# A mixture-of-experts kernel: its table of tokens by slot made by matmuls of zeros and ones in place of scatters, with attention and routing pieces reordered

## The chip, the cores and the metric

The kernel runs on one core of a Trainium2 chip. The metric is the device time of one execution in microseconds (us); the time of a version is the median over its runs. A core has five engines that run their own instruction streams and meet at semaphores: TensorE (PE, matmuls; PEld its weight loads), VectorE (DVE), ScalarE (ACT), GpSimd (POOL) and SyncE (SP, which mostly issues DMAs). An engine takes its instructions strictly in its own order.

## The reference

Three layers follow each other on B = 2 sequences of S = 768 tokens with 8 heads of 40. The first is a gated recurrent attention, computed here in chunks of 128 tokens. The second sends each token to 2 of 8 experts, the third adds four experts over all tokens:

```python
logits = x @ w_gate
noisy_logits = logits + np.log1p(np.exp(x @ w_noise)) * noise
top2 = np.argpartition(-noisy_logits, 2, axis=1)[:, :2]
...
for e in range(E):                       # 8 experts, F = 1024
    for k in range(2):
        mask = top2[:, k] == e
        h = np.maximum(x[mask] @ w1[e], 0.0)
        out[mask] += top2_w[mask, k, None] * (h @ w2[e])
...
for e in range(E):                       # 4 experts over all 1536 tokens
    h = np.maximum(x @ w1[e], 0.0)
    out += p[:, e:e + 1] * (h @ w2[e])
```

## The kernel before

**Stages.** Attention runs in 12 chunks, six of each batch. A chunk's row `x` goes to the table `Xall` in DRAM. Its scores `sp`, decays `A`, state update `up` and state `C`, output `hp`, `tp`, `x`, transposes `xp` and routing logits `lp`, `lt` are computed by all the engines in turn: PE makes the products, DVE multiplies scores into A, adds `up` to C and normalises `x`; ACT takes exponentials and copies; POOL masks A (`affine_select`, L335), scales queries (`qg`, L353) and decays C (L368). Routing of a batch (`route`) is done in two halves, h = 0 for its first four chunks and h = 1 for the last two. The first expert layer then runs in units: units 0 to 3 are experts 0 to 3 for the tokens of batch 0 alone (two tiles of 128), unit 4 and those behind it need tokens of batch 1. A unit gathers its tokens from `Xall` (`xload`, POOL indirect DMAs `xe`), transposes them (`prep`, into `pa`, `pb`), splits them into a high and a low part (`xh` on ACT, `xl` on DVE), multiplies by the first weights (L194, result `s`), takes the positive part and splits it (`hh`), and multiplies by the second weights (L208). Weights come as `raw` by SP's DMAs and are split as `w1hi`, `w2hi` on ACT and `w1lo`, `w2lo` on DVE (L174, L175).

**Order.** It is written out by hand in two strings. `PLAN1` mixes, up to unit 0, attention pieces (A, four to a chunk), routing pieces of batch 0 (r), weight splits (w) and single steps (z, o). What is left of routing and splits is then drained, the gathers of units 0 and 1 are issued, and `LEAD` further attention pieces are drained before unit 0 is prepared. `PLAN2` is woven with the matmuls of units 0 to 3, one letter or blank after each group of matmuls: A is the rest of attention, r the routing of batch 1. A scheduler then sets the order of instructions of one piece on the engines.

**The table.** Which token stands in which slot of which expert is known, for each token, as a slot number. `route` writes the number of each token to the DRAM table `Td` at its slot: 8 indirect DMAs by POOL for h = 0 and 4 for h = 1, a yield after each, so that each is an r of its own. After h = 1 SP reads the table back into `tok`, 32 columns of 128, and the gathers take their row numbers from `tok`.

Of the kernel before, what the change touches and what calls it, by code (L numbers as in the profile page):

```python
# [65 lines left out]
def body(ctx: ExitStack, tc: tile.TileContext, d, o, dbg=None):  # L66
    nc = tc.nc
    const = ctx.enter_context(tc.tile_pool(name="const", bufs=1))
# [28 lines left out]
    slot = [const.tile([P, 2, NC], I32, name=f"slot_{b}") for b in range(B)]  # L97
# [6 lines left out]
    Td = dram.tile([NROW, 1], I32, name="Td")  # L104
# [28 lines left out]
    toki = const.tile([P, NT], I32, name="toki")  # L133
    nc.gpsimd.iota(toki, pattern=[[P, NT]], base=0, channel_multiplier=1)
    zidx = const.tile([P, E1 * NCOL], I32, name="zidx")
    nc.gpsimd.memset(zidx, 0)
    dumpi = pro.tile([P, NC, E1], I32, name="dumpi")
    nc.gpsimd.iota(dumpi, pattern=[[P * E1, NC], [P, E1]], base=SPARE, channel_multiplier=1)
    dump = const.tile([P, NC, E1], F32, name="dump")
    nc.gpsimd.tensor_copy(dump, dumpi)  # L140
# [337 lines left out]
    def route(b, h):  # L478
        t = rt[b]
        if h == 0:  # L480
            nl = at.tile([P, NC, E1], F32, name="nl")
            selb = at.tile([P, NC, E1], BF16, name="selb")
            sel = at.tile([P, 2, NC, E1], F32, name="sel")
            t.update(nl=nl, selb=selb, sel=sel, prev=[])
        nl, selb, sel, prev = t["nl"], t["selb"], t["sel"], t["prev"]
# [29 lines left out]
        sl = at.tile([P, 2, HC, E1], F32, name=f"sl{h}")  # L515
# [534 lines left out]
```

## Time and profile before

| | us |
|---|---|
| runs | 710.33, 710.69, 712.83 |
| median | 710.69 |
| the profiled execution | 708.15 |
| its span, first to last instruction | 706.1 |
| PE busy in the span | 680.1 |
| DVE busy | 369.3 |
| ACT busy | 262.1 |
| POOL busy | 126.1 |

The profiled execution is 2.54 us below the median and has 2.05 us outside its span. The clock of PE granted over the span was 0.976 of full speed. Times in the rows below are us from the span's start; the idle time of an engine before an instruction stands in brackets with what ended it.

### The profile page before, as it was taken

To read this page: it belongs to the slowest core of one execution; us is meant where nothing else is said; L and a number is where in the kernel's file an instruction comes from. 1 tells how busy PE (TensorE), PEld (TensorE's weight loads), DVE (VectorE), ACT (ScalarE), POOL (GpSimd) and SP (SyncE) were. 2 spreads that over 40 slices of the span, in tenths; PEclk is the share of its full clock that TensorE was granted. 3 is DMA by queue.
4 is the path that set the end of the run, shared out by engine and by line. 5 is a ranking of instruction groups with operands and counts; after the bars stand their busy time and mean duration, and the time that the engine had idled before them with its cause. 6 is when DMAs were issued, how large, how long until landed. Compare 5 with 4: busy or idle time off the path is not lost.

```text
span 706.1 us, 11386 instructions
## 1 busy us (share of the span) xinstructions
PE 680.1 (96%) x4427; PEld 622.7 (88%) x4427; DVE 369.3 (52%) x787; ACT 262.1 (37%) x501; POOL 126.1 (18%) x183
## 2 busy tenths in 40 slices
PE   9898688999999999999999999999999999999997
PEld 6776577999899999999889899898898998989987
DVE  7868587877565664658756334412444224332141
ACT  5558446763453543545541223302233113121120
POOL 5544572142612101124023000000000000000000
PEclk9998779999999999999999999999999999999999
DMA  6889647665665444567662003100130001001011
GB/s 195 220 246 302 196 115 234 194 202 168 172 195 163 136 135 148 135 189 244 187 189 75 1 19 109 38 1 1 31 103 31 1 1 37 1 1 39 1 37 41
DMA packets 39946, 80.03 MB, mean 113 GB/s; under 512 B 9377, under 2 KB 16465, under 8 KB 39889
## 3 DMA queue, kind: packets, MB, share of 16 engines
q1 hardware_dynamic: 36496, 70.39, 33.2%
q0 software_dynamic: 3392, 8.86, 4.5%
q8 instruction: 37, 0.61, 0.4%
q14 instruction: 21, 0.16, 0.1%
HBM read 70.20 MB, written 9.04 MB: 112 GB/s over the span
## 4 chain that ended last, share of the span: by engine, by line
PE 79%; DMA 10%; DVE 5%; issue 2%; ACT 1%; POOL 1%; SPq 0%; ACTq 0%; DVEq 0%; POOLq 0%
PE z L194 25%; PE z L208 24%; PE s L194 12%; PE s L208 10%; DMA raw<-w 4%; DMA A<-LFd 2%; PE sp L342 1%; PE s L204 1%; DMA raw<-v 1%; DMA Td<-toki,slot 1%; DMA kp<-kT 1%; DVE w2lo L175 1%; PE lp L449 1%; PE hp L407 1%; POOL Td L540 1%
## 5 line engine op out<-in xcount | busy, mean ns | idle before, releaser
L211 ACT ACTIVATE hh<-z 128x512 fp32r<-128x512 f32 x96 | 57.1, 600 | 192.4 <-PE z L194 192.3
L208 PE MATMUL z<-w2hi,hh 128*128 128x320 f32 x384 | 118.6, 309 | 0.0
L208 PE MATMUL z<-w2hi,hl 128*128 128x320 f32 x384 | 118.3, 308 | 0.0
L208 PE MATMUL z<-w2lo,hh 128*128 128x320 f32 x384 | 118.3, 308 | 0.0
L194 PE MATMUL z<-x2h,w1hi 128*128 128x512 f32 x288 | 112.4, 390 | 0.0
L208 PE MATMUL s<-w2hi,hh 128*128 128x320 f32 x448 | 107.6, 312 | 1.7 <-ACT hh L211 0.9
L212 DVE SCALAR_TENSOR_TENSOR hl<-z,hh 128x512 fp32r<-128x512 f32 x96 | 65.8, 690 | 82.5 <-ACT hh L211 82.5
L194 PE MATMUL z<-x2h,w1lo 128*128 128x512 f32 x288 | 96.6, 389 | 0.0
L194 PE MATMUL s<-xh,w1hi 128*128 128x256 f32 (+1 forms) x288 | 84.5, 312 | 3.3 <-ACT xh L186 3.3
L175 DVE TENSOR_TENSOR w2lo<-raw,w2hi 128x640 fp32r<-128x640 f32 x60 | 49.6, 828 | 65.6 <-ACT w2hi L174 65.5
L208 PEld LDWEIGHTS s<-w2hi,hh 128*128 128x128 f32 x448 | 76.7, 188 | 2.8 <-ACT hh L211 1.2
L174 ACT CAST w2hi<-raw 128x640 fp32r<-128x640 f32 x60 | 43.5, 728 | 87.2 <-PE s L204 25.3
L194 PE MATMUL z<-x2l,w1hi 128*128 128x512 f32 x192 | 74.8, 390 | 0.0
L175 DVE TENSOR_TENSOR w1lo<-raw,w1hi 128x768 fp32r<-128x768 f32 x60 | 57.2, 957 | 29.8 <-ACT w1hi L174 29.2
L208 PEld LDWEIGHTS z<-w2lo,hh 128*128 128x128 f32 x384 | 72.1, 188 | 0.6
L208 PEld LDWEIGHTS z<-w2hi,hh 128*128 128x128 f32 x384 | 72.1, 188 | 0.5
L208 PEld LDWEIGHTS z<-w2hi,hl 128*128 128x128 f32 x384 | 72.1, 188 | 0.0
L194 PE MATMUL s<-xh,w1lo 128*128 128x256 f32 (+1 forms) x288 | 70.5, 309 | 0.0
L208 PE MATMUL s<-w2lo,hh 128*128 128x320 f32 x224 | 69.2, 309 | 0.0
L194 PEld LDWEIGHTS z<-x2h,w1lo 128*128 128x128 f32 x288 | 54.1, 188 | 11.3
L174 ACT CAST w1hi<-raw 128x768 fp32r<-128x768 f32 x60 | 49.9, 836 | 36.7 <-PE s L194 15.3
L194 PEld LDWEIGHTS z<-x2h,w1hi 128*128 128x128 f32 x288 | 54.0, 188 | 10.8
(188 smaller groups left out, 1025.0 us busy)
## 6 DMA issues: line engine op xcount, KB each, us to landing
raw<-w SPq DMA_DIRECT2D x44, 384.0 KB
raw<-w SPq DMA_DIRECT2D x44, 320.0 KB
raw<-v SPq DMA_DIRECT2D x16, 384.0 KB
A<-LFd SPq DMA_DIRECT2D x10, 512.0 KB
raw<-v SPq DMA_DIRECT2D x16, 320.0 KB
kv<-kv SPq DMA_DIRECT2D x12, 324.0 KB
Yd<-ys SPq DMA_DIRECT2D x8, 320.0 KB
qt<-qT SPq DMA_DIRECT2D x12, 208.0 KB
```

What stands on the lines that cost most here:

```text
L174: nc.scalar.copy(hi, raw)
L175: nc.vector.tensor_sub(lo, raw, hi.bitcast(F32))
L194: nc.tensor.matmul(out_ps, l, r, start=(i == 0), stop=(i == len(seq) - 1))
L204: nc.tensor.matmul(yp, both[f], r[:, k], start=(f == 0 and i == 0), stop=(f == NF - 1 and i == 1))
L208: nc.tensor.matmul(yp, l, r, start=(f == 0 and i == 0), stop=(f == NF - 1 and i == 2))
L211: nc.scalar.activation(hh, src, AF.Relu)
L212: nc.vector.scalar_tensor_tensor(hl, src, 0.0, hh.bitcast(F32), ALU.max, ALU.subtract)
L342: nc.tensor.matmul(sp[:, j, :], t["kp"][:, 4 * g + j, :], t["qt"][:, j, :], start=True, stop=True)
L407: nc.tensor.matmul(hp[64 * j : 64 * j + 41, p, :], t["kv"][:, 4 * j + p, D:], t["A"][:, 4 * j + p, :], start=False, stop=(p == 3))
L449: nc.tensor.matmul(lp[32 * k : 32 * k + 32], wgn[r, k, :], st[i]["xt"][r, k, :], start=True, stop=True)
L540: s = nc.gpsimd.indirect_dma_start(out=Td, out_offset=bass.IndirectOffsetOnAxis(ap=slot[b][:, k, c : c + 1], axis=0), in_=toki[:, b * NC + ...
```

## The change

The table is made on chip. For each half of a batch, DVE builds a one-hot row over the 128 places of a column (`oh`) for each of the K = 8 or 4 token choices, and a one-hot row over the 32 columns (`in_col`), which it multiplies by the token's partition number and by the token's base (`rh`). K matmuls add the products up in PSUM (`pt`), and two additions put them into `table`; after h = 1 a cast makes `tok`. `Td`, its clearing, the slot cast, the 12 scatters of a batch and the read-back are gone. `sl` and `sf` have a third plane, for the place in the column. `LEAD` is 2 in place of 6, and both plans are rewritten: PLAN1 has 32 A and 21 r in place of 35 and 32, and a letter X at which the gathers of units 0 and 1 are issued; PLAN2 has 23 A and 25 r in place of 20 and 40.

```diff
-LEAD = 6
+LEAD = 2
-PLAN1 = "AAAAAAAAAAAzAAoAAAArrwArAwArrrrrArArrrrwrAAArrrArrArAwrrArArAArrrrArrrArA"
-PLAN2 = "A AA  AA r A AAA r rr rr A  A AA Ar ArrrrrrrrrA Arr r  A rrrr   rr rrrrr rr  r Arr rArr r  r "
+PLAN1 = "AAAAAAAAAAAAAAoAAArArArwArArArwArArrArArwrArrArwrXArArrAr"
+PLAN2 = "AA AA AA AA A    AAr AAr AAr AAr r r r r Ar Ar Ar Ar r r r r Ar Ar rr r r r r r "
...
-        nc.vector.scalar_tensor_tensor(spare, g, 0.0, dump[:, n], ALU.is_ge, ALU.mult)
+        nc.vector.tensor_scalar(spare, g, 0.0, 1000.0, ALU.is_ge, ALU.mult)
...
-        nc.vector.tensor_mul(tmp, sel[:, :, n], sl[:, 0].unsqueeze(1).to_broadcast([P, 2, HC, E1]))
-        nc.vector.tensor_reduce(sf, tmp, AX.X, ALU.add)
-        nc.vector.tensor_copy(slot[b][:, :, n], sf)
-        yield
-        for c in range(c0, c0 + HC):
-            for k in range(2):
-                s = nc.gpsimd.indirect_dma_start(out=Td, out_offset=bass.IndirectOffsetOnAxis(ap=slot[b][:, k, c : c + 1], axis=0), in_=toki[:, b * NC + c : b * NC + c + 1], in_offset=None)
...
-                yield
+        for w in (0, 2):
+            nc.vector.tensor_mul(tmp, sel[:, :, n], sl[:, w].unsqueeze(1).to_broadcast([P, 2, HC, E1]))
+            nc.vector.tensor_reduce(sf[:, w], tmp, AX.X, ALU.add)
+        K = 2 * HC
+        oh = at.tile([P, K, P], BF16, name=f"oh{h}")
+        rh = at.tile([P, 2, K, E1 * NCOL], BF16, name=f"rh{h}")
+        in_col = at.tile([P, K, E1 * NCOL], BF16, name=f"in_col{h}")
+        nc.vector.tensor_tensor(oh, count.unsqueeze(1).to_broadcast([P, K, P]), sf[:, 2].rearrange("p k c -> p (k c)").unsqueeze(2).to_broadcast([P, K, P]), ALU.is_equal)
+        yield
+        nc.vector.tensor_tensor(in_col, count[:, : E1 * NCOL].unsqueeze(1).to_broadcast([P, K, E1 * NCOL]), sf[:, 0].rearrange("p k c -> p (k c)").unsqueeze(2).to_broadcast([P, K, E1 * NCOL]), ALU.is_equal)
+        nc.vector.tensor_scalar(rh[:, 0], in_col, place[:, 0:1], None, ALU.mult)
+        for k in range(2):
+            c = slice(k * HC, (k + 1) * HC)
+            nc.vector.tensor_mul(rh[:, 1, c], in_col[:, c], place[:, 1 + b * NC + c0 : 1 + b * NC + c0 + HC].unsqueeze(2).to_broadcast([P, HC, E1 * NCOL]))
+        yield
+        pt = psum([P, 2, E1 * NCOL], "pt")
+        for i in range(K):
+            nc.tensor.matmul(pt, oh[:, i], rh[:, :, i], start=(i == 0), stop=(i == K - 1))
+        nc.vector.tensor_add(table, table, pt[:, 0])
+        nc.vector.tensor_add(table, table, pt[:, 1])
+        if h == 1:
+            nc.vector.tensor_copy(tok[b].rearrange("p e j -> p (e j)"), table)
+            routed.add(b)
+        yield
...
-        nc.sync.dma_start(tok[b].rearrange("p e j -> p (e j)"), Td[: P * E1 * NCOL].rearrange("(p j) o -> p (j o)", p=P))
```

The places where the order of instructions moves follow, each before and then with the change. The first is POOL's row beside the attention of chunks 8 to 10, where C is the attention state (L368), A the masked decay, qg the scaled queries; in brackets are the semaphores that a row waits for, DMASW those of POOL's own transfers. Before:

```order
L353 TENSOR_TENSOR qg<-qt,gb 104x512 [waits DMAHW5_49,DMAHW6_49,DMAHW3_49,PE_49]
L335 AFFINE_SELECT A<-A 128x512 [waits Activation_49]
L540 DMA Td<-toki,slot_89 10240x1 [waits DVE_49]
L540 DMA Td<-toki,slot_89 10240x1 x7
L335 AFFINE_SELECT A<-A 128x512 [waits DMAHW5_49,PE_49,Activation_49]
L368 TENSOR_TENSOR C_190<-C_188,gb 40x4x41 [waits PE_49]
L368 TENSOR_TENSOR C_190<-C_188,gb 40x4x41 [waits DMASW3_49,DMASW4_49,DMASW2_49,DMASW5_49,DMASW1_49,DMASW6_49,DMASW0_49,DMASW7_49,DVE_49,Pool_49]
```

With the change:

```order
L353 TENSOR_TENSOR qg<-qt,gb 104x512 [waits DMAHW4_49,DMAHW5_49,DMAHW2_49,PE_49]
L335 AFFINE_SELECT A<-A 128x512 [waits Activation_49]
L335 AFFINE_SELECT A<-A 128x512 [waits DMAHW3_49,PE_49,Activation_49]
L368 TENSOR_TENSOR C_190<-C_188,gb 40x4x41 [waits DVE_49,PE_49]
L368 TENSOR_TENSOR C_190<-C_188,gb 40x4x41 [waits DVE_49,Pool_49]
```

The eight scatters are gone from between qg and C, and the second C row no longer waits for transfers of POOL.

The second place is PE's row at chunk 7, from its scores to its output; pt is the new table product. Before:

```order
L342 MATMUL sp_1041<-qt,kp_162 128x128 x4
L449 MATMUL lp_1046<-xt,wgn 32x128 x3
L415 MATMUL tp_1055<-ident,hs 128x105 x4
L400 MATMUL hp_1081<-qg,C_190 105x128 x4
L460 MATMUL lt_1092<-ident,ls 128x96
```

With the change:

```order
L449 MATMUL lp_1040<-xt,wgn 32x128 x3
L553 LDWEIGHTS oh_980
L553 MATMUL pt_1047<-rh_981,oh_980 128x64
...
L415 MATMUL tp_1060<-ident,hs 128x105
L553 LDWEIGHTS oh_980
L553 MATMUL pt_1047<-rh_981,oh_980 128x64
...
L415 MATMUL tp_1060<-ident,hs 128x105 x3
L400 MATMUL hp_1086<-qg,C_190 105x128 x4
```

Eight table matmuls now stand between lp and the last of tp.

The third place is PE's row where the first expert matmul (L194, to `s`) stands. Before, where sp_1429 are scores and hp_1474 the output of chunk 11:

```order
L342 MATMUL sp_1429<-qt,kp_164 128x128 x4
L407 MATMUL hp_1420<-A,kv 41x128 x8
L449 MATMUL lp_1452<-xt,wgn 32x128 x3
L415 MATMUL tp_1459<-ident,hs 128x105 x4
L400 MATMUL hp_1474<-qg,C_190 105x128 x4
L612 MATMUL pa_1483<-ident,xe 128x128 x2
L407 MATMUL hp_1474<-A,kv 41x128 x5
L194 MATMUL s_102_1501<-xh,w1hi 128x256
```

With the change, where sp_1423 are scores of chunk 10 and hp_1371 is the output of chunk 9:

```order
L407 MATMUL hp_1371<-A,kv 41x128 x8
L626 MATMUL pa_1380<-ident,xe 128x128 x2
L627 MATMUL pb_1381<-ident,xe 64x128
L626 MATMUL pa_1380<-ident,xe 128x128 x2
L627 MATMUL pb_1381<-ident,xe 64x128
L194 MATMUL s_90_1398<-xh,w1hi 128x256
L342 MATMUL sp_1423<-qt,kp_162 128x128 x3
L194 MATMUL s_90_1398<-xl,w1hi 128x256
```

The scores of chunk 10 and all of chunk 11 stand behind the first expert matmul here; before, chunks 10 and 11 stood ahead of it but for the last products and transposes of chunk 11.

## Rows read from the trace of the kernel before

**Rows 1.** The page: busy time of each engine, share, instructions.

```profile
PE 680.1 (96%) x4427; PEld 622.7 (88%) x4427; DVE 369.3 (52%) x787; ACT 262.1 (37%) x501; POOL 126.1 (18%) x183
```

**Rows 2.** Windows, 60.4 to 114 us: length, busy time by engine, clock, DMA share, GB/s.

```profile
60.40:71.40 11.00, 10.51 (x93) 8.28 (x91) 10.10 (x35) 8.17 (x20) 5.53 (x6) 0.78 1.00 292
71.40:77.40 6.00, 2.44 (x40) 1.81 (x40) 5.29 (x24) 4.77 (x12) 4.71 (x5) 0.85 0.92 246
77.40:86.00 8.60, 8.60 (x55) 7.28 (x52) 1.75 (x8) 1.54 (x2) 2.66 (x5) 0.51 0.65 208
86.00:100.00 14.00, 9.93 (x67) 8.10 (x63) 12.00 (x47) 6.74 (x21) 10.15 (x14) 0.63 0.28 65
100.00:114.00 14.00, 11.38 (x125) 9.07 (x124) 8.73 (x24) 4.94 (x12) 9.33 (x9) 1.00 0.78 242
sum 53.60, PE 42.86 PEld 34.54 DVE 37.87 ACT 26.17 POOL 32.38; mean PE 8.57 PEld 6.91 DVE 7.57 ACT 5.23 POOL 6.48
```

**Rows 3.** Timeline of POOL: start, length, instruction; in brackets the idle time before it.

```profile
...
68.00 1.22 POOL L540 DMA_INDIRECT Td<-toki,slot  x1 [0.83 <-DVE xt L442]
...
77.63 0.96 POOL L540 DMA_INDIRECT Td<-toki,slot  x1 [0.30 <-issue]
...
85.31 0.47 POOL L368 TENSOR_TENSOR C<-C,gb 40x164 f32<-40x164 f32 x1 [5.63 <-DMA Td<-toki,slot]
...
86.45 1.26 POOL L353 TENSOR_TENSOR qg<-qt,gb 104x512 f32<-104x512 f32 x1
...
```

**Rows 4.** Timeline of VectorE (DVE), 79 to 115 us.

```profile
...
79.71 0.32 DVE L389 TENSOR_TENSOR C<-up,C 40x164 f32<-40x164 f32 x1 [2.18 <-POOL C L368]
...
85.81 0.33 DVE L389 TENSOR_TENSOR C<-up,C 40x164 f32<-40x164 f32 x1 [4.67 <-POOL C L368]
...
86.70 1.04 DVE L526 SCALAR_TENSOR_TENSOR sl<-g,sl 128x16 f32<-128x16 f32 x1
...
114.11 0.69 DVE L187 TENSOR_TENSOR xl<-pa,xh 128x512 fp32r<-128x512 f32 x1 [2.72 <-ACT xh L186]
...
```

**Rows 5.** Timeline of TensorE (PE), 37 to 116 us.

```profile
...
37.69 1.13 PE L342 MATMUL sp<-qt,kp 104*128 104x128 f32 x8 [0.51 <-PE up L376]
...
38.75 0.74 PE L449 MATMUL lp<-xt,wgn 128*32 128x128 f32 x6
...
50.73 0.74 PE L449 MATMUL lp<-xt,wgn 128*32 128x128 f32 x6
...
68.55 0.74 PE L449 MATMUL lp<-xt,wgn 128*32 128x128 f32 x6
...
73.64 0.41 PE L438 MATMUL xp<-ident,x 128*128 128x128 f32 x2 [1.96 <-DVE x L428]
...
77.72 2.08 PE L342 MATMUL sp<-qt,kp 104*128 104x128 f32 x8
...
115.24 0.39 PE L194 MATMUL s<-xl,w1hi 128*128 128x256 f32 x1
...
```

**Rows 6.** Groups of VectorE by line and shape, 0 to 200 us: busy, mean ns.

```profile
...
L175 DVE TENSOR_TENSOR w1lo<-raw,w1hi 128x768 fp32r<-128x768 f32 x21 | 19.9, 957 | 4.9 <-ACT w1hi L174 4.6
...
L500 DVE TENSOR_TENSOR df<-nl 128x256 f32<-128x256 f32 x2 | 0.9, 426 | 0.0
...
L500 DVE TENSOR_TENSOR df<-nl 128x128 f32<-128x128 f32 x2 | 0.6, 292 | 0.1
...
L545 DVE TENSOR_TENSOR tmp<-sel,sl 128x64 f32<-128x64 f32 x2 | 0.4, 212 | 0.0
...
```

**Rows 7.** Groups of TensorE by line and shape, 0 to 180 us.

```profile
...
L514 PE MATMUL pp<-selb,ones 128*128 128x24 bf16 x2 | 0.4, 178 | 0.0
...
```

**Rows 8.** Window of the dense units 0 to 3, columns as in rows 2.

```profile
115.20:181.40 66.20, 65.34 (x508) 63.31 (x505) 50.95 (x140) 37.16 (x62) 18.91 (x19) 1.00 0.63 181
```

**Rows 9.** Timeline of TensorE at the start of unit 4.

```profile
...
180.21 0.44 PE L612 MATMUL pa<-ident,xe 128*128 128x128 f32 x2 [0.25 <-DMA xe<-Xall,tok]
...
181.36 0.73 PE L194 MATMUL s<-xh,w1hi 128*128 128x256 f32 x4 [0.61 <-ACT xh L186]
...
```

More of the change, by code (lines that the diff above doesn't have):

```diff
@@ L27 @@
 NCOL = 4
-SPARE = P * E1 * NCOL
-NROW = SPARE + S * E1
 TINY = 1.1754944e-38
@@ L32 @@
 NQ = 4
-LEAD = 6
+LEAD = 2
 PARTS = [slice(0, 1), slice(1, 2), slice(2, 4), slice(4, NC)]
 WARM = 11
-PLAN1 = "AAAAAAAAAAAzAAoAAAArrwArAwArrrrrArArrrrwrAAArrrArArrAwrrArArAArrrrArrrArA"
-PLAN2 = "A AA  AA r A AAA r rr rr A  A AA Ar ArrrrrrrrrA Arr r  A rrrr   rr rrrrr rr  r Arr rArr r  r "
+PLAN1 = "AAAAAAAAAAAAAAoAAArArArwArArArwArArArrArArwrArrArwrXArArrAr"
+PLAN2 = "AA AA AA AA A    AAr AAr AAr AAr r r r r Ar Ar Ar Ar r r r r Ar Ar rr r r r r r "
 RAW = 3 * F // NQ
@@ L96, in body @@
     wsel = [const.tile([P, 2, NC], F32, name=f"wsel_{b}") for b in range(B)]
-    slot = [const.tile([P, 2, NC], I32, name=f"slot_{b}") for b in range(B)]
     back = [const.tile([P, 2, NC], I32, name=f"back_{b}") for b in range(B)]
@@ L103, in body @@
     psm = const.tile([P, NT], F32, name="psm")
-    Td = dram.tile([NROW, 1], I32, name="Td")
     tok = [const.tile([P, E1, NCOL], I32, name=f"tok_{b}") for b in range(B)]
@@ L132, in body @@
         nc.gpsimd.memset(off[b][:, ALONE:], -float(JCAP))
[L133 to L140, printed above, removed]
+    counti = pro.tile([P, P], I32, name="counti")
+    nc.gpsimd.iota(counti, pattern=[[1, P]], base=0, channel_multiplier=0)
+    count = at.tile([P, P], F32, name="count")
+    nc.gpsimd.tensor_copy(count, counti)
+    placei = pro.tile([P, 1 + NT], I32, name="placei")
+    nc.gpsimd.iota(placei[:, 0:1], pattern=[[0, 1]], base=0, channel_multiplier=1)
+    nc.gpsimd.iota(placei[:, 1:], pattern=[[P, NT]], base=0, channel_multiplier=0)
+    place = at.tile([P, 1 + NT], F32, name="place")
+    nc.gpsimd.tensor_copy(place, placei)
+    table = at.tile([P, E1 * NCOL], F32, name="table")
+    nc.gpsimd.memset(table, 0.0)
     STREAM = []
@@ L483, in route @@
             sel = at.tile([P, 2, NC, E1], F32, name="sel")
-            t.update(nl=nl, selb=selb, sel=sel, prev=[])
-        nl, selb, sel, prev = t["nl"], t["selb"], t["sel"], t["prev"]
+            t.update(nl=nl, selb=selb, sel=sel)
+        nl, selb, sel = t["nl"], t["selb"], t["sel"]
         n = HALVES[h]
@@ L514, in route @@
             nc.tensor.matmul(pp[:, j - c0 :, :], ones, selb[:, j - i : last + 1 - i, :], start=False, stop=(i == last))
-        sl = at.tile([P, 2, HC, E1], F32, name=f"sl{h}")
+        sl = at.tile([P, 3, HC, E1], F32, name=f"sl{h}")
         yield
@@ L526, in route @@
             nc.vector.scalar_tensor_tensor(sl[:, 0], g, float(i * P), sl[:, 0], ALU.is_ge, ALU.add)
-        nc.vector.scalar_tensor_tensor(sl[:, 0], sl[:, 0], float(1 - P * E1 * NCOL), wide(ebase[:, 0]), ALU.mult, ALU.add)
-        nc.vector.scalar_tensor_tensor(sl[:, 0], g, float(E1 * NCOL), sl[:, 0], ALU.mult, ALU.add)
-        nc.vector.tensor_max(sl[:, 0], sl[:, 0], spare)
+        nc.vector.scalar_tensor_tensor(spare, sl[:, 0], -float(P), spare, ALU.mult, ALU.add)
+        nc.vector.tensor_add(sl[:, 2], g, spare)
+        nc.vector.tensor_add(sl[:, 0], sl[:, 0], wide(ebase[:, 0]))
         nc.vector.tensor_add(sl[:, 1], g, wide(ebase[:, 1 + b]))
@@ L532, in route @@
         tmp = at.tile([P, 2, HC, E1], F32, name=f"tmp{h}")
-        sf = at.tile([P, 2, HC], F32, name=f"sf{h}")
-        nc.vector.tensor_mul(tmp, sel[:, :, n], sl[:, 0].unsqueeze(1).to_broadcast([P, 2, HC, E1]))
-        nc.vector.tensor_reduce(sf, tmp, AX.X, ALU.add)
-        nc.vector.tensor_copy(slot[b][:, :, n], sf)
-        yield
-        for c in range(c0, c0 + HC):
-            for k in range(2):
-                s = nc.gpsimd.indirect_dma_start(out=Td, out_offset=bass.IndirectOffsetOnAxis(ap=slot[b][:, k, c : c + 1], axis=0), in_=toki[:, b * NC + c : b * NC + c + 1], in_offset=None)
-                for q in prev:
-                    tc.declare_no_dep(s.ins, q.ins, reason="distinct rows")
-                prev.append(s)
-                yield
+        sf = at.tile([P, 3, 2, HC], F32, name=f"sf{h}")
@@ L545, in route @@
+        yield
[8 more added lines that the diff above has]
+        yield
         nc.vector.tensor_mul(tmp, sel[:, :, n], sl[:, 1].unsqueeze(1).to_broadcast([P, 2, HC, E1]))
-        nc.vector.tensor_reduce(sf, tmp, AX.X, ALU.add)
@@ L547, in route @@
-        nc.vector.tensor_copy(back[b][:, :, n], sf)
+        nc.vector.tensor_reduce(sf[:, 1], tmp, AX.X, ALU.add)
+        nc.vector.tensor_copy(back[b][:, :, n], sf[:, 1])
         yield
@@ L907, in body @@
     nc.sync.dma_start(noise, d["noise"])
-    def init():
-        nc.sync.dma_start(Td[: P * E1 * NCOL].rearrange("(p j) o -> p (j o)", p=P), zidx)
     def routes(b):
@@ L914, in routes @@
             yield from route(b, h)
-        routed.add(b)
     def splits():
@@ L925, in body @@
     for w in PLAN1:
-        if w in "zo":
-            init() if w == "z" else og_load(1)
+        if w == "o":
+            og_load(1)
+        elif w == "X":
+            xload(0)
+            xload(1)
         else:
@@ L931, in body @@
     drain(R0)
-    xload(0)
-    xload(1)
     drain_n(A, LEAD)
```

## The prediction

> **What bounds the kernel now.** I read four views in this order. The table of engines [rows 1]: TensorE is busy 680.1 of 706.1 us and VectorE 369.3, so a change can only pay where TensorE stands idle or slow. The windows [rows 2] say where: up to about 115 us attention, routing and weight splitting run together, and TensorE is busy 42.86 of 53.6 us, at a granted clock of 0.78, 0.85, 0.51, 0.63 and then 1.00 (between its levels of 2.4 and 1.2 GHz). From the first dense expert matmul at 115.24 [rows 5] it is busy 65.34 of the next 66.2 us [rows 8], and so to the end nearly. So whatever brings that start forward is kept, unless later units lose it again. The reader should take the whole question as: when does the first expert's dense stretch start, and what work has been done by then?
>
> The timelines say what holds it. POOL issues eight scatters from 68.00, the last at 77.63, and its second decay of C waits 5.63 us for them to land, until 85.31 [rows 3]. VectorE's additions to C wait behind POOL: 2.18 and 4.67 us, 6.85 in all [rows 4]. Everything later in VectorE's row is queued behind them. At the end of the stretch xl waits 2.72 us more for ACT's xh [rows 4], which stands behind a weight split that waits for its raw data.
>
> **The change, part by part. First, the waits removed.** No scatter is left on POOL, so its C has no landing to wait for, and VectorE's 6.85 us go. What is late next is whatever in VectorE's row is not ready when it comes earlier. I keep every other wait of that row: VectorE is idle 53.6 - 37.87 = 15.7 us [rows 2]; 6.85 is the POOL wait, 14.0 - 8.73 = 5.3 lies in the last window (the 2.7 for xh included), so 3.6 us stay.
>
> **Second, new VectorE work, on the path.** Per batch the change adds to VectorE two comparisons against slots (128x1024 and 128x512), two against columns (128x256, 128x128), six products, two extra multiply-and-sum pairs, four table additions and a cast, and drops two casts and some steps of the slot formula. From [rows 6]: 128x256 takes 0.426, 128x768 0.957, so about 1.04 ns an element, and 1024 elements come to 1.22 and 512 to 0.69; 128x256 twice 0.85; 128x128 at 0.292 four times 1.17; 128x64 at 0.212 for the other two products 0.42; the pairs, the additions and the cast, some 11 small instructions at no more than that, less about 6 dropped, 1.0. Sum 5.35, taken as 5.3; bounds 4.3 (the bf16 results halve the two large ones) and 6.6 (two of them held up as below). Nothing hides this in batch 0: VectorE is the engine that the others wait for.
>
> **Third, work moved.** In the new order LEAD is 2 and the attention of chunks 10 and 11 stands behind the first expert matmul, woven between groups of 16; before, nearly all of it stood ahead. On VectorE that is, instruction for instruction, the content of the last window, 8.73 us [rows 2]. On TensorE it is some 1.7 of its chunk steps; at full clock a step takes (50.73 - 38.75) / 2 = 6.0 us [rows 5], so 10.1 us. It is moved, not saved, so the start must be compared with 114.1 - 10.1 = 104.0.
>
> **The sum for the start.** VectorE from 60.4: 37.87 - 8.73 + 5.3 = 34.4 of work and 3.6 of waits, so xl at 98.4 against 104.0: **-5.6**. Bounds: without any wait 94.8, so -9.2; the other end is TensorE's clock. In the new order the eight table matmuls of the first half stand in TensorE's row between lp and tp of chunk 7. lp is at 68.55 [rows 5]; by adding up VectorE's row the second product is ready at about 72.3, so TensorE idles some 3 us. In the trace it was granted 0.51 after such idling (2.44 busy of 6.0 us, then 8.60 of 8.60 at 0.51 [rows 2]), and eight sp matmuls took 2.08 us in place of 1.13 [rows 5]. If all that is left (chunk 7 from here, chunk 8 and three quarters of chunk 9, some 15.8 us at 6.0 a step) runs at the low level: 72.3 + 15.8 x 2.08 / 1.13 = 101.4, with transposes and xh 102.3, so -1.7. I take VectorE's number, since the wait for the table is likely to be shorter than its bound.
>
> **Fourth, VectorE beside POOL.** A slot step of 128x16 took 1.04 us while POOL's qg ran, 1.26 us from 86.45 [rows 3, 4]; both ended together. One of the new comparisons in batch 0 may be caught so; I take half of one, **+0.6** (0 to 2.6). The Trainium skill, SBUF — State Buffer, section SBUF: two separate sides, says that a VectorE instruction with two SBUF inputs and a GpSimd one that reads SBUF hold their shared ports in turn for the whole instruction; that row agrees with it. By that rule every new comparison and product is exposed, for each reads two SBUF tiles, and the term would lie towards its upper bound: a rule against this change.
>
> **Fifth, TensorE in batch 1.** Its 12 table matmuls stand in a saturated stretch. The nearest row is a bf16 matmul of 128x24, 178 ns alone [rows 7]; pipelined with a weight load I put 0.1 each, **+1.2** (0.5 to 2.1). Its VectorE work of 5.3 and the 8.73 moved fall where VectorE was busy 50.95 of 66.2 us [rows 8]: 65 of about 77.5, covered on average.
>
> **Sixth, unit 4,** the first that needs batch 1. Its transposes and matmuls lost 0.25 + 0.61 us before it ran evenly [rows 9]; without scatters and read-back its tokens come sooner: **-0.9** (0 to -0.9). **Seventh, the weaving:** attention in the dense stretch waits on VectorE as it always did, for example 1.96 us at xp [rows 5], with groups of some 2 us of dense matmuls between: **+0.5** (0 to 4). POOL's C of chunk 10 now waits for the landing of four gathers, but the transposes ahead of the first dense matmul wait for the first two of them, so little is left. The raw weight loads, spread over steps, and the larger constants on POOL before 10 us cost nothing that another wait doesn't cover.
>
> Sum: -5.6 + 0.6 + 1.2 - 0.9 + 0.5 = **-4.2 us** on the profiled execution's 708.15, so 703.95. The median of the three runs is 2.54 higher, 710.69; the forecast for it is **706.5**.
>
> **Rivals.** (A) The forecast, chance 0.44. (B) *The clock holds.* With the gaps of 75 to 90 us gone TensorE stays near 2.4 GHz, and VectorE runs without its last 3.6 us of waits: -9.2 + 0.6 + 1.2 - 0.9 = -8.3, 702.4. For it: the low clock followed idle stretches. Against: the new wait for the table. Chance 0.18. (C) *The landing was covered anyway, so the change does nothing.* In 77.4 to 86.0, while VectorE waited, TensorE was busy all 8.60 us, at 0.51 [rows 2]. If the low clock is entered at the new table wait, the path is TensorE's: -1.7 + 0.6 + 1.2 - 0.9 + 0.5 = -0.3, 710.4. Chance 0.23. (D) *The other side: the woven attention stalls the dense units.* TensorE takes its row strictly in order, so each attention matmul that is not ready stops the expert matmuls behind it, and hh and the weight splits of the unit now share VectorE with the attention, the table and batch 1's routing. Two chunks meet VectorE about six times (xp, tp, hp of each); at 1.96 each that is 11.8, in place of 0.5: -4.2 + 11.3 = +7.1, 717.8; it turns slower than before from three such waits. Against it: the covering groups, and VectorE's 65 of 77.5. Chance 0.15.
>
> **How the numbers follow.** A change of under 0.5% (3.6 us) can't be told from none here. The range leaves out the worse part of D and a little of B: low 700.5, high 712. Faster: most of A (its own range 703.5 to 708.5), all of B, a little of C and D, 0.60; same: the rest of A and most of C, 0.26; slower: most of D, 0.14.
>
> **What would show it.** Right: no POOL wait for a scatter, VectorE idle in 77 to 86 us below 2 us, the first dense matmul at 97 to 101 us, four gathers issued near 90, unit 4 starting some 4 us earlier. The clock of 75 to 100 tells B from C: 1.0 or 0.5; a wait of tp or pt for oh of 3 us speaks for C. In 100 to 180, TensorE idle over 4 us with waits of xp, tp, s on VectorE is D. I am wrong if the first dense matmul comes after 103, or if unit 4 starts later than 179.

## The result, and the profile after

The changed kernel takes 716.97 us (median of six runs, 714.88 to 718.84) against 710.5 us (six runs, 708.37 to 712.83): a ratio of 1.009, 95% interval [1.0061, 1.0118]. It is **0.9% slower**; forecast were 706.5 us and at most 712. The profiled execution took 717.05 us with a span of 715.3, so the two traces differ by 9.2 us in span where the medians differ by 6.5. The six runs of one kernel lie up to 4.5 us apart, and a difference between two traces is only that exact.

The table of engines after, to be held against [rows 1]:

```profile
PE 683.5 (96%) x4451; PEld 625.3 (87%) x4451; DVE 375.7 (53%) x821; ACT 262.7 (37%) x501; POOL 102.3 (14%) x161
```

POOL lost 24 us of scatters, VectorE gained 6.4, TensorE has 24 small matmuls and 3.4 us more. None of that is 9 us. The loss is found by cutting both traces at the same three events: the first routing product `pp` of batch 0, the first transposes `pa` of unit 0, and the first `pa` of unit 4, the first unit that needs batch 1. All moved pieces lie between the first and the third. Windows of before, columns as in [rows 2]:

```profile
61.36:109.84 48.48, 40.30 (x344) 33.20 (x344) 35.69 (x128) 24.92 (x61) 30.17 (x34) 0.75 0.66 189
109.84:179.47 69.63, 66.94 (x525) 64.64 (x524) 52.74 (x143) 38.93 (x65) 19.57 (x19) 1.00 0.66 194
```

The same two stretches after:

```profile
61.47:101.22 39.75, 31.25 (x256) 25.31 (x256) 32.23 (x124) 20.86 (x52) 17.27 (x19) 0.71 0.75 222
101.22:186.75 85.53, 78.24 (x637) 73.40 (x636) 63.43 (x180) 43.75 (x74) 12.36 (x13) 0.99 0.59 168
```

Read the second line of each first. TensorE is busy 78.24 - 66.94 = 11.30 us more there: the twelve table matmuls of batch 1 are 1.03 of it and the moved attention the rest, 10.3; forecast were 1.2 and 10.1. But its idle time in the stretch grew from 2.69 to 7.29 us, +4.60. Of the 2.69 before, all was one wait of unit 0 for `xh`, of which 0.52 is left; 3.04 of the 7.29 are waits for the table of batch 1 and 3.72 are waits of the woven attention. The first line: the start is 8.73 us shorter, but 10.1 us of work (the forecast's count) left it, so at equal work it is 1.4 us *longer*. Its idle time is 8.50 us where it was 8.18, though the landing wait is gone. The trace's list of what TensorE waited for after (engine, line, releaser: us in all, times, longest) names the new first entry:

```profile
PE pt L553 <- DVE rh L549: 10.1, 5, 4.0
PE xp L438 <- DVE x L428: 2.7, 4, 1.0
PE sp L342 <- DMA A<-LFd: 2.4, 1, 2.4
PE lp L449 <- ACT xt L441: 2.0, 1, 2.0
```

TensorE's timeline shows where these waits stand; rows of before at the same places are in [rows 5]:

```profile
...
68.14 0.41 PE L449 MATMUL lp<-xt,wgn 128*32 128x128 f32 x4
...
73.08 0.40 PE L553 MATMUL pt<-rh,oh 128*128 128x64 bf16 x4 [3.98 <-DVE rh L549]
...
74.29 1.92 PE L400 MATMUL hp<-qg,C 104*105 104x128 f32 x8
...
89.19 0.29 PE L553 MATMUL pt<-rh,oh 128*128 128x64 bf16 x2 [2.69 <-DVE rh L549]
...
93.45 2.08 PE L342 MATMUL sp<-qt,kp 104*128 104x128 f32 x8
...
103.28 0.39 PE L194 MATMUL s<-xh,w1hi 128*128 128x256 f32 x1 [0.52 <-ACT xh L186]
...
136.05 0.41 PE L438 MATMUL xp<-ident,x 128*128 128x128 f32 x2 [0.45 <-DVE x L428]
...
140.53 0.41 PE L449 MATMUL lp<-xt,wgn 128*32 128x128 f32 x4 [2.04 <-ACT xt L441]
...
155.10 0.28 PE L553 MATMUL pt<-rh,oh 128*128 128x64 bf16 x4 [2.70 <-DVE rh L549]
...
```

Nothing of attention is late when the first stop begins, at 69.1 us: TensorE stops because the table's matmuls are next in its row and VectorE has not made their operands. Not all of that is the table's work. VectorE's row has two weight splits among the table's steps, the second just ahead of the last product:

```profile
...
69.54 0.95 DVE L175 TENSOR_TENSOR w1lo<-raw,w1hi 128x768 fp32r<-128x768 f32 x1
...
71.87 0.95 DVE L175 TENSOR_TENSOR w1lo<-raw,w1hi 128x768 fp32r<-128x768 f32 x1
72.74 0.48 DVE L549 TENSOR_TENSOR rh<-in_col,place 128x128 bf16<-128x128 bf16 x2
...
```

They put the last product off by 0.87 us each, 1.7 of the 3.98; no run has them behind it. After the second stop, at 89.19, the eight `sp` matmuls at 93.45 take 2.08 us, as after the gaps of before, and the granted clock over 71.4 to 77.4 and 86 to 100 us is low again (the third number from the end, a mean of the two levels, 1.00 and 0.50 of 2.4 GHz):

```profile
71.40:77.40 6.00, 4.32 (x27) 4.30 (x28) 4.64 (x17) 1.45 (x5) 3.49 (x3) 0.54 0.62 204
77.40:86.00 8.60, 7.28 (x82) 5.50 (x82) 7.96 (x37) 4.58 (x9) 2.53 (x4) 0.92 0.46 137
86.00:100.00 14.00, 10.95 (x75) 8.76 (x73) 10.31 (x41) 6.01 (x19) 8.00 (x11) 0.61 0.85 231
```

VectorE is busy 7.96 of the 8.60 us in which it waited before [rows 2]. POOL's row shows why, and that its landing wait is not wholly gone:

```profile
...
85.50 1.05 POOL L368 TENSOR_TENSOR C<-C,gb 40x164 f32<-40x164 f32 x2 [5.99 <-PE lt L460]
...
89.03 1.26 POOL L353 TENSOR_TENSOR qg<-qt,gb 104x512 f32<-104x512 f32 x1
...
102.30 0.47 POOL L368 TENSOR_TENSOR C<-C,gb 40x164 f32<-40x164 f32 x1 [1.90 <-DMA xe<-Xall,tok]
...
```

The C that stood 5.63 us for scatters [rows 3] no longer waits for any transfer; the C of chunk 10 now waits 1.90 us for the gathers issued ahead of it.

### The profile page after: what moved, and what is told of

It is laid out like the page before. It is cut to its first block, busy times and chain, and to the rows that moved or that the text cites. A ratio compares the mean times of both kernels' runs of the same rounds, so it can differ in the third digit from the quotient of the medians.

```text
span 715.3 us, 11425 instructions
## 1 busy us (share of the span) xinstructions
PE 683.5 (96%) x4451; PEld 625.3 (87%) x4451; DVE 375.7 (53%) x821; ACT 262.7 (37%) x501; POOL 102.3 (14%) x161
## 4 chain that ended last, share of the span: by engine, by line
PE 83%; DMA 6%; DVE 5%; ACT 3%; issue 2%; POOL 0%; SPq 0%; ACTq 0%; POOLq 0%; DVEq 0%
PE z L194 24%; PE z L208 24%; PE s L194 13%; PE s L208 10%; PE sp L342 3%; DMA raw<-w 2%; DMA A<-LFd 1%; PE s L204 1%; DMA raw<-v 1%; ACT w1hi L174 1%; PE hp L407 1%; PE pa L626 1%; DVE w1lo L175 1%; DVE w2lo L175 1%; PE lp L449 1%
## 5 line engine op out<-in xcount | busy, mean ns | idle before, releaser
L194 PE MATMUL z<-x2h,w1hi 128*128 128x512 f32 x288 | 112.4, 390 | 0.0
L208 PE MATMUL s<-w2hi,hh 128*128 128x320 f32 x448 | 109.1, 316 | 2.6 <-DVE hh L212 1.4
L194 PE MATMUL z<-x2h,w1lo 128*128 128x512 f32 x288 | 96.6, 389 | 0.0
L194 PE MATMUL s<-xh,w1hi 128*128 128x256 f32 (+1 forms) x288 | 85.3, 313 | 1.9 <-ACT xh L186 1.9
L194 PE MATMUL z<-x2l,w1hi 128*128 128x512 f32 x192 | 74.8, 390 | 0.0
L194 PE MATMUL s<-xh,w1lo 128*128 128x256 f32 (+1 forms) x288 | 70.4, 308 | 0.0
L194 PEld LDWEIGHTS z<-x2h,w1lo 128*128 128x128 f32 x288 | 54.1, 188 | 11.3
L194 PEld LDWEIGHTS z<-x2h,w1hi 128*128 128x128 f32 x288 | 54.0, 188 | 10.8
```

The lines of the kernel that those rows point to most:

```text
L194: nc.tensor.matmul(out_ps, l, r, start=(i == 0), stop=(i == len(seq) - 1))
L208: nc.tensor.matmul(yp, l, r, start=(f == 0 and i == 0), stop=(f == NF - 1 and i == 2))
```

## Experiments

Two theories at first. **T**: the loss is TensorE's wait for the table. **W**: it is the new order, with attention woven between the dense matmuls. Each run is compared with runs of the kernel before on the same chip, whose median there was 706.3 to 709.5 us, so ratios are compared, not medians. In the column of the table, "at once" is the change's way (each half's matmuls with that half's routing), and "late" is all of them with the second half's. "Start" is from the first `pp` to unit 0's transposes, "units 0 to 3" from there to unit 4's, both from the one profiled execution.

| run | order | table | besides | median us | ratio to before | start | units 0 to 3 |
|---|---|---|---|---|---|---|---|
| before | old | scatters | | 710.5 | 1 | 48.5 | 69.6 |
| after | new | at once | | 716.97 | 1.009 [1.0061, 1.0118] | 39.8 | 85.5 |
| e1 | new | scatters | | 726.87 | 1.0234 [1.0128, 1.034] | 48.9 | 85.2 |
| e2 | new | at once | LEAD 6 | 720.36 | 1.0128 [1.0039, 1.0216] | 47.0 | 88.2 |
| e3 | new | late | | 716.62 | 1.0091 [1.005, 1.0132] | 37.0 | 86.8 |
| e4 | old | late | | 719.51 | 1.0134 [1.0048, 1.022] | 51.6 | 74.2 |
| e5 | old | late | batch 1's routing earlier | 714.15 | 1.0075 [1.0047, 1.0103] | 52.0 | 71.8 |
| e6 | all attention first | at once | | 727.41 | 1.0258 [1.0206, 1.0311] | 59.4 | 75.7 |
| e7 | new | at once | 5 raw buffers | 712.30 | 1.0068 [1.0035, 1.01] | 40.9 | 82.8 |
| e8 | old | scatters | 5 raw buffers | 705.74 | 0.9956 [0.9915, 0.9997] | 48.0 | 68.2 |
| e9 | old | late | e5, gathers behind C | 707.67 | 1.0025 [0.9982, 1.0067] | 47.2 | 70.2 |
| e10 | old | late | e9, 5 raw buffers | 710.02 | 1.0046 [1.0006, 1.0086] | 47.0 | 72.7 |
| e11 | old | at once | e5, gathers behind C | 714.39 | 1.0148 [1.0051, 1.0246] | 53.2 | 73.1 |
| e12 | new | late | 5 raw buffers | 715.18 | 1.0125 [1.0082, 1.0168] | 37.6 | 86.6 |

**e1: the order alone.** The kernel before with the new LEAD and plans, the letters of clearing and scatters put back where the new table pieces stand:

```diff
-LEAD = 6
+LEAD = 2
-PLAN1 = "AAAAAAAAAAAzAAoAAAArrwArAwArrrrrArArrrrwrAAArrrArrArAwrrArArAArrrrArrrArA"
+PLAN1 = "AAAAAAAAAAAAAAzoAAArArArwArArArwArrrrArrrrArrArArwrArrArrwrrArArrAr"
```

> The scatters of the kernel before, with the changed kernel's order (LEAD 2, both plans; the scatters of a half are issued where the table's pieces stood, the gathers of units 0 and 1 after the last routing piece). Theory T (the table's matmuls stand on TensorE ahead of their data: 3.98 and 3.05 us in batch 0, 2.70 us in batch 1): those waits are gone and POOL's wait for the landing is back, so about the kernel before, 708 to 712 us. Theory W (the attention woven into units 0 to 2 stalls the dense work, whatever makes the table): the loss of about 3.7 us at 133 to 145 us stays, and POOL's wait is back as well, so 715 to 720.

Slower than either theory said: 2.3%. TensorE stands 7.97 us at unit 0's transposes for the gathers, which wait for scatters and read-back, and the start gains nothing although 10.1 us of work left it:

```profile
...
109.45 0.66 PE L612 MATMUL pa<-ident,xe 128*128 128x128 f32 x2 [7.97 <-DMA xe<-Xall,tok]
...
```

So in the new order the table made on chip is worth about 10 us (1.0234 to 1.009; e1's four runs lie between 722.06 and 731.56). It isn't the table against the scatters as such that loses.

**e2: LEAD 6 in the changed kernel,** the attention pieces that it takes removed from PLAN2.

```diff
-LEAD = 2
+LEAD = 6
-PLAN2 = "AA AA AA AA A    AAr AAr AAr AAr r r r r Ar Ar Ar Ar r r r r Ar Ar rr r r r r r "
+PLAN2 = "  AA AA A    AAr AAr AAr AAr r r r r Ar Ar Ar Ar r r r r Ar Ar rr r r r r r "
```

> The changed kernel with LEAD 6 again and the first four attention pieces taken from the second plan, so that chunk 10 is done ahead of unit 0. Theory T: the waits for the table stay, 715 to 718. Theory W: with less attention in the units the stall at 133 to 145 us goes or shrinks, 711 to 714.

W's gain did not come: 720.36. In its profiled execution, which at 725.44 is the slowest of the four, the three waits for the table stay (3.98, 2.68, 2.71), and one of 3.69 at an `lp` comes in, behind a weight split on ACT that waited 2.86 us for raw data.

**e3: the table's matmuls late.** Those of the first half are issued with the second half's, so TensorE doesn't meet them at chunk 7:

```diff
-        pt = psum([P, 2, E1 * NCOL], "pt")
-        for i in range(K):
-            nc.tensor.matmul(pt, oh[:, i], rh[:, :, i], start=(i == 0), stop=(i == K - 1))
-        nc.vector.tensor_add(table, table, pt[:, 0])
-        nc.vector.tensor_add(table, table, pt[:, 1])
+        t[f"ohs{h}"] = [(oh[:, i], rh[:, :, i]) for i in range(K)]
+        if h == 1:
+            pt = psum([P, 2, E1 * NCOL], "pt")
+            terms = t["ohs0"] + t["ohs1"]
+            for i, (l, r) in enumerate(terms):
+                nc.tensor.matmul(pt, l, r, start=(i == 0), stop=(i == len(terms) - 1))
+            nc.vector.tensor_add(table, table, pt[:, 0])
+            nc.vector.tensor_add(table, table, pt[:, 1])
```

> The changed kernel, but the eight table matmuls of the first half are issued with the four of the second, into one sum, so that no matmul of the first half waits for VectorE; two table additions a batch fall away. Theory T: the waits of 3.98 and 2.70 us go, and with them some of the low clock, 708 to 711. Theory W: the start is hardly earlier, or the woven attention loses it again, 714 to 717.

The wait of 3.98 went, the start is 2.8 us shorter, and the time is the same, as W said. What came instead stands in e12 below, which repeats it with a fifth raw buffer.

**e4, e5: the late table in the order of before.** LEAD is 6, and both plans are those of before without the letters of scatters (e4: first line); in e5 the second batch's routing letters stand earlier (second and third line: PLAN2 of e4, then of e5). In e5, and in e9 to e11 which build on it, the gathers of batch 1 are also held until units 0 to 3 are through (`routed.add(1)` stands there):

```diff
+PLAN1 = "AAAAAAAAAAAAAoAAAArrwArAwArrrrrAAwAAArrrArArrAwrrArAAArrrArAAX"
-PLAN2 = "A AA  AA r A AAA r rr rr A  A AA Ar Ar      rrA Arr r  A rrrr      rrrr        A    A        "
+PLAN2 = "A AA  AA r A AAA r rr rr A  A AA Ar Ar rrA Arr r  A rr rr rr rr           A    A        "
```

> The table made on chip, its matmuls issued late as in the third run, in the order of the kernel before (its two plans without the scatter pieces, LEAD 6, gathers after the routing). Theory T: neither a wait for the table in the first half nor POOL's wait for the landing, 705 to 709; by theory W too, since almost no attention is woven into the units, 704 to 708. A time of 710 or more says that the table itself costs what the landing cost.

> The fourth run again, whose units 0 to 3 lost nothing but whose gathers of batch 1 waited until 181.85 us for a count that stood on VectorE behind a copy of results (5 us idle at unit 4, then low clock): now batch 1's routing pieces come some six steps earlier. If that wait was all that the fourth run lost: 719.5 - 9 to 12, that is 706 to 711, with the first dense matmul near 112 and unit 4 at 178 to 180. If the table made on chip costs more than that: 713 or more.

If only the order were at fault, both should have been at or below before. They aren't, and POOL's row in e5 says what neither theory held:

```profile
...
98.04 0.95 POOL L616 DMA_INDIRECT xe<-Xall,tok  x1 [0.30 <-issue]
99.00 0.48 POOL L368 TENSOR_TENSOR C<-C,gb 40x164 f32<-40x164 f32 x1
105.08 0.46 POOL L368 TENSOR_TENSOR C<-C,gb 40x164 f32<-40x164 f32 x1 [5.60 <-DMA xe<-Xall,tok]
...
```

With TensorE's timeline of e5 behind it:

```profile
...
107.30 0.63 PE L449 MATMUL lp<-xt,wgn 64*32 64x128 f32 x2 [7.26 <-DVE xt L442]
...
```

The second C behind a set of POOL's own indirect DMAs carries waits for their semaphores, as the order of before showed for the scatters. With the scatters gone, the gathers are that set: VectorE waits for C, and TensorE for VectorE. (In e4 batch 1's routing is late as well: unit 4's gathers are issued only from 181.85.)

**e6: all attention ahead of unit 0.**

```diff
-LEAD = 2
+LEAD = 40
-PLAN2 = "AA AA AA AA A    AAr AAr AAr AAr r r r r Ar Ar Ar Ar r r r r Ar Ar rr r r r r r "
+PLAN2 = "                   r   r   r   r r r r r  r  r  r  r r r r r  r  r rr r r r r r "
```

> The changed kernel with all attention issued ahead of unit 0 (nothing of it woven into the units; the second plan's A letters are blanks). Theory W (weaving costs the 3.7 us at 133 to 145 us): units 0 to 3 run with less idle time on TensorE than 7 us, unit 0 starts 10 to 14 us later, 712 to 717. Theory that the weave hides waits of the attention: the start is more than 15 us later, 720 or more.

W in its plain form falls: without any weaving it is 2.6% slower. Units 0 to 3 take 75.7 us with no attention in them, and TensorE stands 4.68 us for the table of batch 1 and 5.26 for unit 4's gathers. In this kernel weaving hides more than it costs.

**e7, e8: a fifth raw weight buffer,** in the changed kernel and in the one before. In the changed one the stop at 140.53 hangs on a late weight load, as ACT's timeline shows:

```profile
...
138.26 0.73 ACT L174 CAST w2hi<-raw 128x640 fp32r<-128x640 f32 x1 [4.94 <-DMA raw<-w]
138.89 0.59 ACT L211 ACTIVATE hh<-s 128x512 fp32r<-128x512 f32 x1
139.38 0.82 ACT L174 CAST w1hi<-raw 128x768 fp32r<-128x768 f32 x1
140.10 0.37 ACT L441 COPY xt<-xp 128x256 f32<-128x256 f32 x1
...
```

`xt`, for which TensorE stands, is queued behind a split whose data came late, because VectorE, waiting 1.41 us for a woven `tp`, had read out its raw buffer late; so I read it, and a fifth buffer tests whether the late load is the cause.

```diff
-        raw = wp.tile([P, RAW], F32, tag="raw", name="raw", bufs=4)
+        raw = wp.tile([P, RAW], F32, tag="raw", name="raw", bufs=5)
```

> The changed kernel with five buffers for raw weights in place of four. If the stall of 133 to 145 us comes from the raw weights that arrive late (w2hi waits 4.94 us for one, and the attention's copy behind it), it goes: 711 to 714. If the row order on ScalarE and VectorE makes it, whatever the weights do: 715 to 718.

> The kernel before with five raw buffers, the control of the seventh run. Its xh stood behind a split that waited 3.37 us for raw weights at 112 us, and 2.7 us of TensorE with it; with another buffer that wait may go: 706 to 709. No change: 709 to 711.

With five buffers the split waits 0.28 us in place of 4.94, that `lp` has no wait left, and units 0 to 3 are 2.7 us shorter: the late load held it. Why the load was late is read from the rows and not tested. On the whole time the intervals of e7 and of the changed kernel overlap. e8 is the fastest kernel here, 0.4% below before, with an interval that ends just under 1.

**e9 to e12.** e9 is e5 with unit 0's and unit 1's gathers queued behind POOL's decay of C for chunk 10, where `cg` holds those instructions:

```diff
     drain_n(A, LEAD)
+    with tc.issue_after(cg[NT - 2].ins):
+        xload(0)
+        xload(1)
```

e10 adds the fifth buffer. e11 is e9 with the matmuls issued half by half, the edit of e3 undone. e12 is e3 with five buffers.

> Late table, the order of before, early second routing, as in the run that gave 714.15 us; here the gathers of units 0 and 1 are issued behind POOL's decay of C for chunk 10 instead of ahead of it. G (POOL's decay of C waited for its own gathers to land, 5.60 us, and TensorE 7.26 us behind it): the wait goes, the first dense stretch starts 4 to 7 us earlier, 707 to 710 us. U (the gathers then land late and unit 0's transposes wait in the place of C, so nothing is won): 713 to 715 us, with a wait of pa for xe of 3 us or more.

> The run before with five raw weight buffers instead of four. If the fifth buffer is worth here what it gave the kernel before and the changed kernel (1.6 to 4.7 us): G gives 703 to 707 us, faster than both kernels; U gives 709 to 713 us.

> As the first run of this set, but the eight table matmuls of the first half stand right behind the slots' product, as in the changed kernel, and not with the second half's four. T (TensorE, in strict order, stands idle for VectorE's table work and is then granted a low clock): a wait of pt for rh of 3 to 4 us in batch 0, and 3 to 6 us slower than the first run of this set. N (TensorE's idle time there is given back later, because VectorE is the engine that the others wait for): within 1.5 us of it.

> The changed kernel with both: the late table matmuls and five raw weight buffers, in the new order. If the two add up (the late table gave 0 to 3 us, the fifth buffer 4.7): 708 to 712 us, and 4 to 7 us more than the kernel before with five buffers (705.74): the rest then lies in the order. If the order isn't it: 705 us or less.

e9: G, at 707.67, and unit 0's transposes don't wait for the gathers. POOL's row: C with 0.98 us of wait, and the gathers behind it.

```profile
...
94.60 0.46 POOL L370 TENSOR_TENSOR C<-C,gb 40x164 f32<-40x164 f32 x1 [4.69 <-PE hp L402]
96.04 0.46 POOL L370 TENSOR_TENSOR C<-C,gb 40x164 f32<-40x164 f32 x1 [0.98 <-DVE C L391]
96.94 1.17 POOL L618 DMA_INDIRECT xe<-Xall,tok  x1 [0.44 <-POOL C L370]
...
```

e9's interval holds 1: in the order of before, with the first half's stop gone and POOL not standing for the gathers, a table made on chip costs and gains nothing that can be told. TensorE still waits 3.4 us for `rh` there, 2.08 of them in batch 1. e5 ran on another chip, and the intervals of e5 and e9 overlap, so for e9 the two waits are shown to be gone, and the gain in the whole time is likely but not shown. e10: a miss, no gain from the fifth buffer. Its profiled execution waits longer for the table of batch 1 than e9's, and has units 0 to 3 at a granted clock of 0.98 instead of 1.00:

```profile
...
164.43 0.22 PE L558 MATMUL pt<-rh,oh 128*128 128x64 bf16 x2 [3.61 <-DVE rh L551]
...
```

e11 beside e9 is the cleanest pair: the same chip and order, and only the place of the first half's eight matmuls in each batch differs (with two small table additions more per batch). It costs 6.7 us, a little more than T expected (714.39 against 707.67; 713.82 to 722.63 against 701.72 to 710.78, so no run of the one lies among the other's). The wait itself is 6.92 us where 3 to 4 were expected. TensorE's timeline of e11:

```profile
...
62.70 0.22 PE L516 MATMUL pp<-selb,ones 128*128 128x24 bf16 x3
69.84 0.61 PE L555 MATMUL pt<-rh,oh 128*128 128x64 bf16 x8 [6.92 <-DVE rh L551]
...
71.58 1.97 PE L342 MATMUL sp<-qt,kp 104*128 104x128 f32 x8
...
```

Windows of the start and of units 0 to 3 of e9:

```profile
62.58:109.75 47.17, 37.95 (x357) 31.62 (x356) 40.37 (x144) 26.18 (x63) 17.51 (x22) 0.83 0.68 213
109.75:180.00 70.25, 67.59 (x537) 65.05 (x536) 55.08 (x156) 37.77 (x63) 9.77 (x10) 1.00 0.64 183
```

The same of e11, six us longer in the start alone:

```profile
62.65:115.81 53.16, 40.15 (x356) 32.57 (x356) 41.58 (x146) 25.40 (x62) 18.08 (x22) 0.73 0.57 175
115.81:188.93 73.12, 69.16 (x537) 66.45 (x536) 55.83 (x159) 38.45 (x64) 9.73 (x10) 0.98 0.62 186
```

Over both stretches TensorE is idle 16.97 us in place of 11.88 (+5.1), and the same matmuls take 109.31 us in place of 105.54 (+3.8) at the lower clock. T is shown here, in the order of before: price of the stops and price of the clock behind them.

e12: a miss, 715.18. The start is the second shortest of all, and TensorE then stands where it didn't before:

```profile
...
79.89 0.17 PE L510 MATMUL pp<-selb,tri 128*128 128x16 bf16 x1 [3.32 <-DVE selb L505]
...
100.04 0.55 PE L629 MATMUL pa<-ident,xe 128*128 128x128 f32 x2 [3.09 <-DMA xe<-Xall,tok]
...
101.87 0.47 PE L629 MATMUL pa<-ident,xe 128*128 128x128 f32 x1 [1.06 <-DMA xe<-Xall,tok]
...
```

In the new order the attention that used to run while table and gathers were under way is behind unit 0, so a later table shows up as a wait for the gathers, and the units begin at a low clock (0.94 over units 0 to 3). So I read why e3 gained nothing: T and W are both partly right, and they don't add. How much of the changed kernel's loss each of them makes is not settled by these runs.

## Why the prediction was wrong

The prediction's terms, against the two traces (its sum was made on the profiled execution):

| term | forecast | found |
|---|---|---|
| start, to the first `xl`: waits removed, table made, work moved; VectorE beside POOL | -5.6 + 0.6 | 103.26 - 104.0 = -0.7 |
| table matmuls of batch 1 | +1.2 | busy 1.0, waits for `rh` 2.7 + 0.3: +4.0 |
| weaving, from the first `xl` to unit 4's transposes | +0.5 | 83.5 - 65.4 - 10.1 - 4.0 = +4.0 |
| unit 4 (to unit 7's transposes) | -0.9 | 58.47 - 58.96 = -0.5 |
| not forecast: behind unit 7 | 0 | +2.4 |
| sum | -4.2 | +9.2 |

The start ends here at the first `xl`, as in the prediction's sum (114.11 less 10.1 of moved work before), and not at the transposes, as in the windows above.

**The step that failed** is in "The sum for the start": "I take VectorE's number, since the wait for the table is likely to be shorter than its bound." VectorE's work was about right: 34.4 us forecast, 33.6 found from 60.4 to its first xl. (The 5.3 a batch of new work were rather too many: over the whole span VectorE gained 6.4 for both batches. The bf16 results did not halve the two large comparisons, as the lower bound had it: 1.22 and 0.68 us.) Its waits were not: 3.6 forecast, 42.9 - 33.6 = 9.3 found, and the row of VectorE after shows for whom it waits, on the way to an xl at 103.26 in place of 98.4:

```profile
...
76.40 0.21 DVE L461 TENSOR_REDUCE lg<-lt 128x16 f32<-128x48 f32 x1 [0.97 <-PE lt L460]
...
97.83 0.17 DVE L422 TENSOR_SCALAR rd<-tp 128x8 f32<-128x8 f32 x1 [1.98 <-PE tp L415]
...
99.46 0.21 DVE L461 TENSOR_REDUCE lg<-lt 128x16 f32<-128x48 f32 x1 [0.63 <-PE lt L460]
...
103.26 0.69 DVE L187 TENSOR_TENSOR xl<-pa,xh 128x512 fp32r<-128x512 f32 x1 [1.43 <-ACT xh L186]
...
```

TensorE stood for VectorE's table, then ran slow, and VectorE stood for TensorE. The bound was there (3 us of idleness, the low clock behind it, -1.7); the wait found is 3.98 at that place, beyond the bound, and a second one of 2.69 for the second half's four matmuls was not counted at all. By xl the start gained 104.0 - 103.26 = 0.7; at the transposes it was still 1.4 behind, since before 4.27 us lay between the two, 2.72 of them the wait at xh [rows 4], and after 2.04. For the start this is rival C's mechanism, which had 0.23, and its clock reading (0.54 and 0.61 in 71 to 77 and 86 to 100 us) was the test that the prediction named. Both of the prediction's signs of being wrong came: the first dense matmul at 103.28 and unit 4 at 186.75.

The stop is not the whole miss of the start. From the first `pp` to the first xl the forecast makes 37.0 us (98.4 less 61.4); the changed kernel took 41.8, and e3 and e12, which have no stop for the first half, 40.0 and 40.8. There VectorE waits at xl instead, behind the transposes that wait for the gathers (rows of e3, then of e12):

```profile
104.49 0.69 DVE L187 TENSOR_TENSOR xl<-pa,xh 128x512 fp32r<-128x512 f32 x1 [3.03 <-ACT xh L186]
103.27 0.69 DVE L187 TENSOR_TENSOR xl<-pa,xh 128x512 fp32r<-128x512 f32 x1 [4.92 <-ACT xh L186]
```

So taking the stop away is worth 1.0 to 1.8 of the 4.8 us that the start missed. The sum has no term for the landing of the gathers ahead of the transposes, and that wait comes up as soon as the table's stop goes; how the rest divides stays open.

**Second step: "covered on average".** The fifth part let VectorE's 65 of 77.5 us cover the table of batch 1. TensorE's row is strict, so an average covers nothing: the matmuls came up at 152 us, their operands were ready at 155.10, and 2.70 us went.

**Weaving** was mis-sized: +0.5 forecast, +4.0 found, the upper end of its bounds (0 to 4). So rival D, nearest in time at 717.8, had a real part of the loss and the wrong size of it: it put 11.8 us on six waits of 1.96, and the woven attention waits 3.72 us in all, at most 2.04 at once. That its number came so near is luck, since the table's waits and the time behind unit 7 made up the rest. The waits became 0.45, 2.04 and 0.61 and two smaller ones, and the largest was not one for VectorE but for ACT, behind a late raw load that the prediction had said cost nothing that another wait doesn't cover.

**POOL's C behind the gathers** was named and dismissed ("so little is left"). In the changed kernel that holds, 1.90 us off the path; in the order of before, with the table late, it is 5.60 us on it (e5), and 0.98 for another cause in e9.

**Right:** the scatters' landing wait went, VectorE is idle only 0.64 us in 77.4 to 86.0, the moved work is 10.3 us (10.1 forecast), the table matmuls 0.1 each. The comparison of 1024 elements took 1.22 us as estimated:

```profile
...
70.73 1.22 DVE L543 TENSOR_TENSOR oh<-count,sf 128x1024 bf16<-128x1024 f32 x1
...
88.49 1.89 DVE L549 TENSOR_TENSOR rh<-in_col,place 128x64 bf16<-128x64 bf16 x2
...
```

The last row is the fourth part's case. The same pair takes 0.35 us in batch 1; here its two instructions took 0.65 us beside POOL's A of 88.27 and 1.32 beside its qg of 89.03, and ended with qg:

```profile
L549 DVE TENSOR_TENSOR rh<-in_col,place x2: 648/984/1319, 88.5 to 89.1; 128x64 bf16<-128x64 bf16 x2
```

They are the half's last operands, so 0.4 of TensorE's 2.69 us hang on the first; the second cost it 0.36 more, since two score products stood between. The term's bounds (0 to 2.6) held, and it is not what decided. The rule that the prediction cited against the change (the Trainium skill, SBUF — State Buffer, section SBUF: two separate sides, the shared ports held for the whole instruction) agrees with these rows: both inputs lie in SBUF.

**Left open.** The 2.4 us behind unit 7 are in this one execution: from unit 7 to the end it takes 470.1 us, the twelve kernels of the experiments 466.5 to 468.8 and before 467.7, so I take them for scatter, which one trace can't show; without them the two traces differ by 6.8 us, near the medians' 6.5. How the loss divides between the table's stops, the gathers and the woven attention is open, since no run takes them away one by one in the new order. The fifth buffer helped in e7 and e8 and not in e10 and e12; why was not settled. No version was found with the table on chip that is faster than before by more than can be told.

## What to carry to other kernels

When an edit moves work from a DMA onto engines, look at the engine that consumes the result in order: matmuls of a side task that stand in TensorE's row ahead of ready work stop everything behind them until the last operand is there, and then the granted clock was low as well (6.7 us here for the place of eight matmuls in each of two batches). Issue them where their operands are sure to be ready, and keep enough independent work between them, the transfer that they feed and its consumer. After taking one landing wait from a queue, look for the next transfer ahead of the same instruction, since it can inherit the wait (5.63 us behind scatters before, 5.60 behind gathers in e5).

## What the hardware showed unexpectedly

The gathers land late: in e5 the last is issued by 98.99 us, and the C that waits for all four starts at 105.08, 6.1 us on. The Trainium skill, DMA: Bandwidth & Descriptors, section Anatomy of one DMA — SWDGE (gpsimd) path, gives about 2.0 us of fixed time per DMA. The time in e5 is three times that, beside the weight loads (the DMA engines were busy 0.71 of the time from 99 to 105.1 us), and the measurement decides.

In e11 the clock granted was 0.50, the lower level, from 60 to 72 us, with TensorE busy 2.92 and 2.16 of 6 us each, and 0.81 over the next 6 us, busy throughout. In e9, without the stop, it was 0.50 from 60 to 66 us too, and 0.82 already from 66 to 72, with TensorE busy 6.00 and 4.35 of 6 us.
